# Attention with experts: five token tables instead of one, and the high parts of keys and queries copied on another engine

## The chip, the core and the metric

The kernel runs on one core of a Trainium2 chip. The metric is the device time of one launch in microseconds (us). TensorE is called PE here (its weight loads PEld), VectorE DVE, ScalarE ACT, GpSimd POOL and SyncE SP. All engines work their own instructions in order; they meet through semaphores.

## What is computed

Attention with rotary position encoding over 8 batches and 8 heads (576 tokens, head width 64) makes a table of 4608 tokens by 512. A gate picks one of 8 experts for each token, and each token goes through its expert's two layers.

```python
B, H, S, D = 8, 8, 576, 64
q_rot, k_rot = rotate(q), rotate(k)
attn = softmax(q_rot @ k_rot.T / sqrt(D))
x = (attn @ v).transpose(0, 2, 1, 3).reshape(B * S, H * D)     # 4608 x 512
e_idx = argmax(x @ w_gate, axis=1)                             # one of 8 experts
for e in range(8):
    mask = e_idx == e
    ye = maximum(x[mask] @ w1[e], 0) @ w2[e]                   # 512 -> 1024 -> 512
    out[mask] = gate_w[mask] * sigmoid(x @ w_output_gate)[mask, e] * ye
```

## The kernel before

**Attention** goes through 32 pairs of heads, four pairs to a batch. A pair has nine steps; a step makes the scores of 128 queries against 576 keys on PE (`scores`), their maximum on DVE (`peak`), the exponential on ACT (`exp`), and one step later a transpose on DVE (`turn`). The global step number is `g`; pair n has steps 9n to 9n+8. Everything else is placed at a step by the table `EVENTS`, written by hand: an entry (name, offset, slot) of pair n is issued at step 9n + offset, in slot 1 (behind the step's exponential) or slot 2 (behind its transpose). The code is issued in that order, so it is also the order on each engine.

To get ready, pair n needs: its keys and queries (`load`, one DMA of 1152 KB into the buffer `raw`, two of them); the rotation (`mult1` and `add1` for keys, `mult0` and `add0` for queries, on POOL); and a split of each into a high part, rounded to the matmul's type (`keyhi`, `queryhi`: a copy), and a low part (`keylo`, `querylo`: the difference). In the kernel before, copy and difference both run on POOL. The high and low keys are `kh` and `kl`, and `q` holds both parts of the queries. A pair's buffer `raw` comes free for the load of pair n+2 when `querylo` has read it. The values are loaded with four DMAs a pair (`loadv`), and the products with the values (`av0` to `av3`) run on PE one pair later.

**Placing.** When a batch's four pairs are done, `place` runs the gate for its 576 tokens as a list of small pieces, one a step, mostly on POOL: it writes the tokens' rows to the DRAM table `xd` (piece `s13`, eight DMAs of SP), counts them by expert, works out for each token its place in the expert's list (`pi`, piece `s17`), and writes the token's number there: five indirect DMAs of POOL (`scatter`, one for each chunk of 128 tokens, the last of 64) into the DRAM list `lst`, 36864 entries filled with a large number at the start. Since the five write one tensor, each waits for the one before to land. In the kernel before, an empty piece stands behind each scatter, so they are two steps apart.

**Experts** (`Moe`). Tokens are handled in slots of 256 or 128 tokens of one expert; the first five slots are taken from the first batches, before all tokens are placed. Three tables of slots (0, 2, 1) are made by `slots`: it works out which rows of 128 entries of `lst` a slot reads, gathers them with one indirect DMA of POOL into `tk` (a row without a token holds the large number), turns `tk` on PE (`tr`) and keeps the token numbers (`idx`). Slot s then gathers its tokens' rows `xg` from `xd` (POOL), turns them, and runs both layers; its weights are loaded by SP and split into high and low parts (`wh` on ACT, `wl` on DVE or POOL). The last batch's `place` and the tables 2 and 1 are issued in pieces between the first slots' matmuls, two pieces to each eighth of a slot, and `gather(s + 2)` stands at the seventh eighth of slot s.

Of the kernel before, what the change touches and what calls it, by code (L numbers as in the profile page):

```python
# [10 lines left out]
F32 = mybir.dt.float32  # L11
# [4 lines left out]
ALU = mybir.AluOpType  # L16
# [6 lines left out]
E, FF = 8, 1024  # L23
P = 128
# [3 lines left out]
NCH = 5  # L28
# [3 lines left out]
BIG = float(1 << 22)  # L32
# [3 lines left out]
NB, TAIL, PO = S // 32, 160, 192  # L36

EVENTS = [
    ("load", -18, 1), ("mult1", -13, 1), ("add1", -11, 1), ("mult0", -10, 1), ("add0", -9, 1), ("key", -8, 1),
    ("query", -6, 2), ("lasts", 1, 2), ("loadv", 1, 2),  # L40
    ("av0", 10, 1), ("av1", 12, 1), ("av2", 14, 1), ("av3", 16, 1),
    ("den", 10, 2), ("evict", 16, 2), ("newxb", 17, 1), ("back", 17, 1), ("divide", 17, 2),
]
# [66 lines left out]
def body(ctx, tc, nb, offs, qk, v, rope, cst, gates, w, out):  # L110
    nc = tc.nc
    NT = nb * S

    def pool(st, n, b, **k):
        return st.enter_context(tc.tile_pool(name=n, bufs=b, **k))


    early, main, scores = ExitStack(), ExitStack(), ExitStack()
    cpool = pool(ctx, "cpool", 1, side="left")
    dpool = pool(ctx, "dpool", 1, space=bass.MemoryType.DRAM)  # L120
    px, px2 = pool(ctx, "px", 1, side="left"), pool(ctx, "px2", 2, side="left")
    pa2 = pool(main, "pa", 2, side="left")
    pp1, pp2 = pool(early, "pp", 1, side="right"), pool(early, "pp2", 2, side="right")
    ps_a = pool(main, "ps_a", 1, space=PSUM, side="left")
    ps_s = pool(scores, "ps_s", 2, space=PSUM, side="right")

    small = Small(ps_s)
    pools = px, px2, pa2, pp1, pp2, ps_s, small, ps_a

    xd = dpool.tile([NT, XW], F32, name="xd")  # L130
    nl = E * list_rows(nb)
    lst = dpool.tile([nl, 1], F32, name="lst")

    first = Pair.first(tc, pools, qk[0, 0], rope)
    ident = cpool.tile([P, P], F32, name="ident")
    make_identity(nc, ident)
    o = offs[C_TRI]
    ct = cpool.tile([P, o], F32, name="ct")
    cc = lambda i: ct[:, offs[i]:offs[i + 1]]

    stage = pa2.tile([P, 2, S], F32, tag="stage", name="stage", bufs=1).rearrange("p a b -> p (a b)")
    nst = offs[-1] - o
    sc = lambda i: stage[:, offs[i] - o:offs[i + 1] - o]

    ii = cpool.tile([P, NP, 2, HW], F32, name="ii")
    trib = cpool.tile([P, P], BF16, name="trib")
    oneb = cpool.tile([P, P], BF16, name="oneb")
    cnt = cpool.tile([P, E], F32, name="cnt")
    zero, big = stage[:, nst:nst + 256], stage[:, nst + 256:nst + 256 + nl // P]
    nc.vector.memset(zero, 0.0)  # L150
    nc.vector.memset(big, BIG)
    nc.scalar.dma_start(out=ct, in_=cst[:, 0:o])
    nc.scalar.dma_start(out=stage[:, 0:nst], in_=cst[:, o:])
    nc.scalar.dma_start(out=ii[:, :, :, D:], in_=gates)

    def consts():
        for h in range(2):
            nc.vector.tensor_copy(ii[:, :, h, 0:D], ident[:, h * D:h * D + D].unsqueeze(1).broadcast_to((P, NP, D)))
        nc.vector.tensor_copy(trib, sc(C_TRI))
        nc.vector.tensor_copy(oneb, sc(C_ONE))  # L160
        nc.vector.memset(cnt, 0.0)
        nc.sync.dma_start(out=lst.rearrange("(p n) o -> p (n o)", p=P), in_=big)

    att = Attention(tc, nb, pools, cc, ident, ii, first, trib, oneb, cnt, zero, qk, v, xd, lst)
    n0 = slot_counts(nb)[0]
    moe = Moe(tc, nb, (px, px2, small), cc, ident, cnt, w, xd, lst, out)

    if n0:
        g = att.done(nb - 3) + 1
        for k, f in enumerate(pieces(moe.table0(), 14)):  # L170
            att.at(g + k, 2, f)
        att.at(att.done(nb - 2) - att.nplace + 22, 2, moe.fetch)
    att.start(consts)
    for g in range(att.G):
        att.step(g)
    early.close()
    if n0:
        moe.open_right(pool(ctx, "mr", 1, side="right", reuse_waits="tile"))
        moe.begin0()
    for g in range(att.G, att.G + TURN):  # L180
        att.step(g)
    scores.close()
    small.move(pool(ctx, "ps_x", 2, space=PSUM, side="right", reuse_waits="tile"))
    if not n0:
        att.rest(lambda g: True)
        main.close()
        moe.open_right(pool(ctx, "mr", 1, side="right", reuse_waits="tile"))
        left = []
    else:
        att.rest(lambda g: g <= att.G + 7)  # L190
        moe.begin1()
        att.rest(lambda g: True)
        main.close()
    moe.open_left(pool(ctx, "ml", 1, side="left", reuse_waits="tile"),
                  pool(ctx, "ps_m", 1, space=PSUM, side="left", reuse_waits="tile"))
    if n0:

        a, b, n = att.last, pieces(moe.table1(), 60), len(att.last) - 10
        left = a[:n] + [lambda f=f, g=g: (f(), g()) for f, g in zip(a[n:], b)] + b[10:]
    else:  # L200
        for f in att.last + pieces(moe.table1(), 60):
            f()
        moe.fetch()
        moe.begin0()
        moe.begin1()
    moe.run(left)


def pieces(gen, n):

    return [lambda: next(gen, None) for _ in range(n)]


class Attention:


    def __init__(self, tc, nb, pools, cc, ident, ii, first, trib, oneb, cnt, zero, qk, v, xd, lst):
        nc = tc.nc
# [10 lines left out]
        for i in range(2):  # L229
            o = (pp1.tile([P, 2, P], F32R, name=f"bd{i}"), px.tile([P, 2 * NCH], F32, name=f"z{i}"),  # L230
                 px.tile([P, 2 * NCH], F32, name=f"rz{i}"))
# [18 lines left out]

        for n, pr in enumerate(self.pairs):
            g, b = 9 * n, n // NP
            fs = {"load": pr.load, "key": pr.key, "query": pr.query, "lasts": pr.lasts, "loadv": pr.loadv, "den": pr.den, "evict": pr.evict, "back": pr.back,
                  "newxb": lambda pr=pr, b=b: newxb(b) if pr.hp == 0 else None}
            fs["divide"] = lambda pr=pr, b=b: pr.divide(xbs[b])
            for t in range(2):
                fs[f"mult{t}"] = lambda pr=pr, t=t: pr.mult("P", t)
                fs[f"add{t}"] = lambda pr=pr, t=t: pr.add("P", t)
            for k, (b0, b1) in enumerate(PIECES):
                fs[f"av{k}"] = lambda pr=pr, b0=b0, b1=b1: [pr.values(j) for j in range(b0, b1)]  # L260
            for name, o, k in EVENTS:
                if n > 1 or name not in ("load", "mult1", "add1", "key", "mult0", "add0", "query")[:7 if n == 0 else 1]:
                    at(g + o, k, fs[name])
            if n % NP == NP - 1:
                fs = place(tc, (px, px2, small), b, NT, cc, trib, oneb, cnt, xbs, xd, lst)
                self.nplace = len(fs)
                if b == nb - 1:
                    self.last = fs
                else:
                    for k, f in enumerate(fs):  # L270
                        at(g + PLACE + k, 2, f)
# [43 lines left out]
class Pair:  # L315
# [79 lines left out]
    def keylo(self, eng):  # L395
        self.sub(eng, self.kl, self.raw[:, 2, :], self.kh.bitcast(F32))

    def key(self):
        self.keyhi("P")
        self.keylo("P")  # L400

    def queryhi(self, eng, x=slice(0, S)):
        if x.start == 0:

# [6 lines left out]
    def lasts(self):  # L411

        for h in range(2):
            r = slice(h * D, h * D + D)
            self.nc.scalar.copy(self.bd[r, :, r], self.q.bitcast(F32)[r, :, QM:S])

    def query(self):
        self.queryhi("P")
        self.querylo("P")

    def begin(self):
        self.pc, self.ps, self.m = {}, {}, {}
# [95 lines left out]
def place(tc, pools, b, NT, cc, trib, oneb, cnt, xbs, xd, lst):  # L518

    nc = tc.nc  # L520
# [3 lines left out]
    V = nc.vector if last else nc.gpsimd  # L524
    tt = V.tensor_tensor
    b3 = lambda t: t.unsqueeze(2).broadcast_to((P, NCH, E))
    T = {}
# [94 lines left out]
    def scatter(c):  # L622
        m = QR if c == 2 else P
        nc.gpsimd.indirect_dma_start(  # L624
            out=lst[:, :], out_offset=bass.IndirectOffsetOnAxis(ap=T["pi"][:m, c:c + 1], axis=0),
            in_=T["tok"][:m, c:c + 1], in_offset=None, bounds_check=E * list_rows(NT // S) - 1, oob_is_err=False)

    def both(f, c):
# [2 lines left out]
    if last:  # L631
        fs = [s0, s1, s2, s3, s4, s5, s6, s7, s8, both(s9, 1), both(s10, 2), both(s11, 3), both(s12, 4), s13, s14, s15, s16, s17]
# [3 lines left out]
        fs = [s0, s1, s2, no, no, s3, no, no, s4, s5, s6, s7, no, no, s8, both(s9, 1), both(s10, 2), both(s11, 3),  # L636
              lambda: add(4), no, no, s12, s13, no, no, s14, s15, no, no, s16, s17]
    for c in range(NCH):
        fs += [lambda c=c: scatter(c), lambda: None]
    return fs  # L640


class Moe:
# [24 lines left out]
    def t(self, sh, n, dt=F32):  # L668
        return self.p1.tile(sh, dt, name=n)
# [14 lines left out]
    def slots(self, n, m, ends, delta, first, step, wait):  # L684
# [19 lines left out]
        if first is not None:  # L704
            V.tensor_tensor(out=row, in0=row, in1=first, op=ALU.add)

        tk = t([m, P], f"{n}tk")
        V.memset(tk, BIG)
        yield
        V.tensor_copy(ri, row)  # L710
        yield
        self.nc.gpsimd.indirect_dma_start(
            out=tk, out_offset=None, in_=self.lst.rearrange("(r c) o -> r (c o)", c=P),
            in_offset=bass.IndirectOffsetOnAxis(ap=ri[0:m, :], axis=0), bounds_check=E * self.rows - 1, oob_is_err=False)
        for _ in range(wait):
            yield
        tr = self.small.tile(f"{n}tr2")
        idx = self.idx[n] = t([P, m], f"{n}idx", I32)
        self.nc.tensor.transpose(out=tr[:, 0, 0:m], in_=tk, identity=self.ident[0:m, 0:m])
# [331 lines left out]
```

## Time and profile before

| | |
|---|---|
| time, median of 3 runs (lowest to highest) | 1294.99 us (1290.09 to 1308.81) |
| profiled execution: its time, and its span | 1298.8 us, 1296.9 us |
| mean granted TensorE clock | 0.889 |
| busy: PE, DVE, ACT, POOL | 1096.8, 838.9, 605.7, 622.8 us |
| attention (first scores to last product) | about 23 to 764 us of the span |
| experts | about 768 us to the end |

The profile's span is the stretch of the profiled execution that its instructions cover. A wait is put down to the instruction of another engine that came last; "issue" is a wait for nothing that the profile shows. A row of the timeline has start, duration (us), engine, line, operation and its tiles, the count, and in brackets the idle time before it and what ended it. A row of the windows has the stretch, and for each engine its busy time and count, then PE's granted clock, the share of 16 DMA engines that was busy, and the GB/s.

### The profile page before, as it was taken

The page shows a single profiled execution, that of the slowest core. Times are in us where ns is not written, and L with a number is a line of the kernel's source. Part 1 is how long each engine was busy: PE and PEld are TensorE (multiplying, and loading weights), DVE is VectorE, ACT ScalarE, POOL GpSimd, SP SyncE. Part 2 cuts the span into 40 slices and gives each one's busy share as a digit, 9 for nine tenths or more (in the row PEclk, how much of TensorE's full clock was granted, in tenths as well). Part 3 has the DMA queues.
Part 4 walks back from the last instruction along what each step waited for, and adds up shares of the span by engine and source line. Part 5 has one row for each costly group of instructions (what it writes and reads, how often), then busy time and mean ns, then how long its engine had stood idle before and what let it go on. Part 6 is the DMA issues. An engine that isn't in the chain of part 4 may idle for free.

```text
span 1296.9 us, 34609 instructions
## 1 busy us (share of the span) xinstructions
PE 1096.8 (85%) x14419; PEld 932.1 (72%) x14419; DVE 838.9 (65%) x1295; ACT 605.7 (47%) x1247; POOL 622.8 (48%) x570
## 2 busy tenths in 40 slices
PE   3988977887886886987985879829999999999998
PEld 2777766675765665765764668628988898989897
DVE  6888855664775674764674546616667767676784
ACT  2455533433443432442432433414557667676674
POOL 6766746636847646656645022122224334363342
PEclk9999977877998887886777779859999999999999
DMA  7454865863865945855852878956668878888891
GB/s 233 126 149 112 120 127 92 114 130 60 146 138 111 143 80 110 125 98 111 116 106 38 108 210 96 249 126 218 208 203 318 267 238 309 292 282 295 278 338 44
DMA packets 88288, 216.19 MB, mean 167 GB/s; under 512 B 48157, under 2 KB 48444, under 8 KB 80064
## 3 DMA queue, kind: packets, MB, share of 16 engines
q1 hardware_dynamic: 78880, 194.18, 62.5%
q0 software_dynamic: 7776, 18.94, 4.8%
q8 instruction: 115, 1.88, 0.8%
q10 hardware_dynamic: 1472, 0.82, 0.2%
q14 instruction: 45, 0.37, 0.1%
HBM read 195.89 MB, written 20.11 MB: 167 GB/s over the span
## 4 chain that ended last, share of the span: by engine, by line
PE 48%; issue 13%; DMA 10%; POOL 6%; DVE 5%; ACT 1%; POOLq 0%; DVEq 0%; ACTq 0%
PE py L928 14%; PE ph L900 11%; PE acc L482 8%; DMA lst<-tok,pi 7%; PE sc L442 7%; PE ph L890 4%; PE acc L501 2%; POOL raw L383 2%; DVE pt L463 2%; POOL lst L624 1%; PE mtp L872 1%; DVE m L448 1%; DMA out<-y,0idx 1%; DVE wl L858 1%; PE sc L435 1%
## 5 line engine op out<-in xcount | busy, mean ns | idle before, releaser
L457 ACT ACTIVATE pm<-sc,m 128x576 f32<-128x576 f32 x288 | 213.2, 740 | 327.5 <-DVE m L448 324.5
L448 DVE TENSOR_REDUCE m<-sc 128x1 f32<-128x576 f32 x288 | 213.9, 743 | 170.1 <-PE sc L442 113.9
L482 PE MATMUL acc<-pt,v 32*64 32x128 f32 (+1 forms) x9216 | 256.9, 331 | 76.7 <-issue 44.0
L858 DVE TENSOR_TENSOR wl<-wr,wh 128x1024 fp32r<-128x1024 f32 x183 | 251.6, 1386 | 72.5 <-ACT wh L856 70.7
L482 PEld LDWEIGHTS acc<-pt,v 32*64 32x64 f32 x9216 | 194.9, 150 | 120.4 <-issue 69.4
L442 PE MATMUL sc<-kh,q 64*128 64x288 f32 x1024 | 240.0, 358 | 48.5 <-ACT pm L457 19.4
L442 PEld LDWEIGHTS sc<-kh,q 64*128 64x128 f32 x1024 | 169.3, 218 | 95.2 <-ACT pm L457 35.4
L463 DVE STREAM_TRANSPOSE pt<-pm 128x576 f32<-128x576 f32 x288 | 220.5, 766 | 3.9 <-ACT pm L457 2.9
L856 ACT CAST wh<-wr 128x1024 fp32r<-128x1024 f32 x208 | 213.3, 1051 | 19.3 <-DMA wr<-in_w 19.3
L928 PE MATMUL py<-wh,ht 128*128 128x512 f32 x640 | 217.8, 405 | 3.2 <-ACT ht L902 2.2
L900 PE MATMUL ph<-xt,wh 128*128 128x256 f32 x896 | 164.4, 286 | 7.6 <-ACT xb L514 4.5
L383 POOL TENSOR_TENSOR raw<-raw,rt 128x1152 f32<-128x1152 f32 x62 | 164.1, 2647 | 9.8 <-DMA raw<-in_qk 9.0
L900 PEld LDWEIGHTS ph<-xt,wh 128*128 128x128 f32 x896 | 141.3, 193 | 9.8 <-ACT xb L514 4.8
L928 PEld LDWEIGHTS py<-wh,ht 128*128 128x128 f32 x640 | 122.5, 192 | 28.8 <-ACT ht L902 2.4
L928 PE MATMUL py<-wl,ht 128*128 128x512 f32 x320 | 127.3, 398 | 2.8 <-POOL wl L858 2.8
L624 POOL DMA_INDIRECT lst<-tok,pi x40 | 41.4, 1035 | 181.1 <-DMA lst<-tok,pi 177.5
L900 PE MATMUL ph<-xt,wl 128*128 128x256 f32 x448 | 127.5, 285 | 0.0
L442 PE MATMUL sc<-kl,q 64*128 64x288 f32 x512 | 121.0, 326 | 0.0
L858 POOL TENSOR_TENSOR wl<-wr,wh 128x1024 fp32r<-128x1024 f32 x25 | 60.8, 2433 | 89.0 <-ACT wh L856 82.9
L442 PEld LDWEIGHTS sc<-kl,q 64*128 64x128 f32 x512 | 96.7, 220 | 0.0
L387 POOL TENSOR_TENSOR raw<-raw 128x576 f32<-128x576 f32 x62 | 87.8, 1415 | 2.2
L900 PEld LDWEIGHTS ph<-xt,wl 128*128 128x128 f32 x448 | 86.3, 193 | 0.0
(205 smaller groups left out, 1299.5 us busy)
## 6 DMA issues: line engine op xcount, KB each, us to landing
wr<-in_w SPq DMA_DIRECT2D x208, 512.0 KB, 5.4
v<-in_v SPq DMA_DIRECT2D x128, 288.0 KB, 7.6
raw<-in_qk SPq DMA_DIRECT2D x31, 1152.0 KB, 8.5
xd<-xb SPq DMA_DIRECT2D x32, 224.0 KB, 9.9
raw<-in_qk SPq DMA_DIRECT2D x2, 576.0 KB
xd<-xb SPq DMA_DIRECT2D x16, 65.0 KB, 2.7
xd<-xb SPq DMA_DIRECT2D x8, 112.0 KB, 11.4
lst<-tok,pi POOLq DMA_INDIRECT x40, 8.1
```

Of the source, the lines that this page charges most:

```text
L383: self.eng(eng).tensor_tensor(out=rv, in0=rv, in1=self.rt[:, 2 * t:2 * t + 2, x], op=ALU.mult)
L387: self.eng(eng).tensor_tensor(out=r[:, 2 * t, x], in0=r[:, 2 * t, x], in1=r[:, 2 * t + 1, x], op=ALU.add)
L442: nc.tensor.matmul(ps[:, a, :HS], self.q[r, w, c * P:c * P + P], mov[r, a * HS:a * HS + HS], start=(n == 0), stop=(n == 2))
L448: nc.vector.tensor_reduce(self.m[i], ps[:, :, :HS], axis=AX.XY, op=ALU.max, negate=True)
L457: nc.scalar.activation(pe.rearrange("p (a b) -> p a b", a=2), self.ps[i][:, :, :HS], AF.Exp, bias=self.m[i], scale=1.0, accum_out=self.z[: ...
L463: self.nc.vector.transpose(out=self.pt[:, st[0] + 5 * st[1] if st else 4, :], in_=self.pc.pop(i))
L482: nc.tensor.matmul(self.acc[h * D:h * D + D, a, o:o + 32 * n], self.v[r, h, j, :], self.pt[r, u:u + n, 32 * j:32 * j + 32], start=(j == 0) ...
L624: nc.gpsimd.indirect_dma_start(out=lst[:, :], out_offset=bass.IndirectOffsetOnAxis(ap=T["pi"][:m, c:c + 1], axis=0), in_=T["tok"][:m, c:c ...
L856: self.nc.scalar.copy(wh, r)
L858: eng.tensor_tensor(out=wl, in0=r, in1=wh.bitcast(F32), op=ALU.subtract)
L900: nc.tensor.matmul(ph[:, f, :], st[:, dc, fs], mv[:, dc, :], start=(n == 0), stop=(n == 11))
L928: self.nc.tensor.matmul(py[h], st[:, f, hs], mv, start=(f == 0 and n == 0), stop=(f == 7 and n == 2))
```

## The change

The one list becomes five, one for each chunk of a batch; a scatter of chunk c writes list c only. Readers gather the same rows from all five into five tiles and take the least on DVE, since a place that a list does not hold reads as the large number. The five tiles are filled on POOL instead of DVE. The empty piece behind each scatter is gone, so they are one step apart. The copies that make the high parts run on ACT, the differences stay on POOL, and the steps of both are given one by one.

```diff
-    ... ("add0", -9, 1), ("key", -8, 1), ("query", -6, 2), ...
+    ... ("add0", -8, 1), ("kh", -7, 1), ("kl", -6, 1), ("qh", -5, 1), ("ql", -4, 1), ...
...
-    lst = dpool.tile([nl, 1], F32, name="lst")
+    lst = [dpool.tile([nl, 1], F32, name=f"lst{c}") for c in range(NCH)]
...
-        nc.sync.dma_start(out=lst.rearrange("(p n) o -> p (n o)", p=P), in_=big)
+        for l in lst:
+            nc.sync.dma_start(out=l.rearrange("(p n) o -> p (n o)", p=P), in_=big)
...
-            fs = {..., "key": pr.key, "query": pr.query, ...
+            fs = {..., "kh": lambda pr=pr: pr.keyhi("A"), "kl": lambda pr=pr: pr.keylo("P"),
+                  "qh": lambda pr=pr: pr.queryhi("A"), "ql": lambda pr=pr: pr.querylo("P"), ...
...
     def scatter(c):
-            out=lst[:, :], out_offset=bass.IndirectOffsetOnAxis(ap=T["pi"][:m, c:c + 1], axis=0),
+            out=lst[c][:, :], out_offset=bass.IndirectOffsetOnAxis(ap=T["pi"][:m, c:c + 1], axis=0),
...
-        fs += [lambda c=c: scatter(c), lambda: None]
+        fs += [lambda c=c: scatter(c)]
...
-        tk = t([m, P], f"{n}tk")
-        V.memset(tk, BIG)
+        tks = [t([m, P], f"{n}tk{c}") for c in range(NCH)]
+        for tk in tks:
+            self.nc.gpsimd.memset(tk, BIG)
...
-        self.nc.gpsimd.indirect_dma_start(
-            out=tk, out_offset=None, in_=self.lst.rearrange("(r c) o -> r (c o)", c=P), ...
+        for l, tk in zip(self.lst, tks):
+            self.nc.gpsimd.indirect_dma_start(
+                out=tk, out_offset=None, in_=l.rearrange("(r c) o -> r (c o)", c=P), ...
         for _ in range(wait):
             yield
+        tk = tks[0]
+        for o in tks[1:]:
+            V.tensor_tensor(out=tk, in0=tk, in1=o, op=ALU.min)
```

On POOL, at the scatters of the first batch, the order before was this, from the second scatter on (`raw`, `kh`, `kl` and `q` carry buffer numbers; `dd` is a piece of the next batch's gate; L383 and L387 are the rotation's products and sums):

```order
L624 DMA lst<-tok_2226,pi_2514 36864x1
L387 TENSOR_TENSOR raw_2378<-raw_2378 128x576
L383 TENSOR_TENSOR raw_2378<-raw_2378,rt 128x1152
L624 DMA lst<-tok_2226,pi_2514 36864x1
L387 TENSOR_TENSOR raw_2378<-raw_2378 128x576
L361 CAST kh_2738<-raw_2378 128x576
L367 TENSOR_TENSOR kl_2739<-raw_2378,kh_2738 128x576
L624 DMA lst<-tok_2226,pi_2514 36864x1
L543 TENSOR_TENSOR dd_2770<-lgs_2684,mx_2746 128x40
L624 DMA lst<-tok_2226,pi_2514 36864x1
L361 CAST q_2827<-raw_2378 128x576
L367 TENSOR_TENSOR q_2827<-raw_2378,q_2827 128x576
```

With the change POOL has there, from the first scatter on (line numbers of the changed file):

```order
L619 DMA lst_84<-tok_2233,pi_2522 36864x1
L370 TENSOR_TENSOR q_2535<-raw_2073,q_2535 128x576
L386 TENSOR_TENSOR raw_2385<-raw_2385,rt 128x1152
L619 DMA lst_85<-tok_2233,pi_2522 36864x1
L619 DMA lst_86<-tok_2233,pi_2522 36864x1
L390 TENSOR_TENSOR raw_2385<-raw_2385 128x576
L619 DMA lst_87<-tok_2233,pi_2522 36864x1
L386 TENSOR_TENSOR raw_2385<-raw_2385,rt 128x1152
L619 DMA lst_88<-tok_2233,pi_2522 36864x1
L390 TENSOR_TENSOR raw_2385<-raw_2385 128x576
L538 TENSOR_TENSOR dd_2780<-lgs_2697,mx_2753 128x40
L370 TENSOR_TENSOR kl_2777<-raw_2385,kh_2776 128x576
```

The scatters go to five lists and stand closer together, between the rotation's instructions of one pair instead of around it and the split; the two copies (CAST) are gone from POOL.

On ACT, in a pair in the middle of the attention, from the exponential of its third step on (`pm`, `sc`, `m` with the step's number), before:

```order
L457 ACTIVATE pm_2_4317,z_107<-sc_2_4308,m_2_4315 128x576
L457 ACTIVATE pm_3_4333,z_107<-sc_3_4324,m_3_4331 128x576
L457 ACTIVATE pm_4_4388,z_107<-sc_4_4379,m_4_4386 128x576
L457 ACTIVATE pm_5_4400,z_107<-sc_5_4391,m_5_4398 128x576
L457 ACTIVATE pm_6_4450,z_107<-sc_6_4441,m_6_4448 128x576
```

and in the same place with the change:

```order
L452 ACTIVATE pm_2_4321,z_111<-sc_2_4312,m_2_4319 128x576
L362 CAST kh_4323<-raw_3933 128x576
L452 ACTIVATE pm_3_4340,z_111<-sc_3_4331,m_3_4338 128x576
L452 ACTIVATE pm_4_4393,z_111<-sc_4_4384,m_4_4391 128x576
L362 CAST q_4395<-raw_3933 128x576
L452 ACTIVATE pm_5_4407,z_111<-sc_5_4398,m_5_4405 128x576
```

The next pair's two copies now stand behind the third and the fifth exponential.

On POOL, where table 0 (`0tk`, gathered with the row numbers `0ri`) is read during the sixth batch's scatters, stood before, from the fourth scatter on:

```order
L624 DMA lst<-tok_8421,pi_8716 36864x1
L543 TENSOR_TENSOR dd_9001<-lgs_8912,mx_8976 128x40
L712 DMA 0tk<-lst,0ri 10x128
L624 DMA lst<-tok_8421,pi_8716 36864x1
L361 CAST q_9061<-raw_8573 128x576
```

and with the change, from that batch's second scatter on:

```order
L619 DMA lst_85<-tok_8428,pi_8748 36864x1
L619 DMA lst_86<-tok_8428,pi_8748 36864x1
L709 DMA 0tk_8769<-lst_84,0ri 10x128
L709 DMA 0tk_8770<-lst_85,0ri 10x128
L709 DMA 0tk_8771<-lst_86,0ri 10x128
L709 DMA 0tk_8772<-lst_87,0ri 10x128
L709 DMA 0tk_8773<-lst_88,0ri 10x128
L390 TENSOR_TENSOR raw_8600<-raw_8600 128x576
L619 DMA lst_87<-tok_8428,pi_8748 36864x1
```

Five gathers stand behind the third scatter of that batch, ahead of a sum of the rotation and the last two scatters.

More of the change, by code (lines that the diff above doesn't have):

```diff
@@ L38 @@
 EVENTS = [
-    ("load", -18, 1), ("mult1", -13, 1), ("add1", -11, 1), ("mult0", -10, 1), ("add0", -9, 1), ("key", -8, 1),
-    ("query", -6, 2), ("lasts", 1, 2), ("loadv", 1, 2),
[2 rows of a table added]
     ("av0", 10, 1), ("av1", 12, 1), ("av2", 14, 1), ("av3", 16, 1),
@@ L196, in body @@
     if n0:
-        a, b, n = att.last, pieces(moe.table1(), 60), len(att.last) - 10
-        left = a[:n] + [lambda f=f, g=g: (f(), g()) for f, g in zip(a[n:], b)] + b[10:]
+        a, b, n = att.last, pieces(moe.table1(), 60), len(att.last) - NCH
+        left = a[:n] + [lambda f=f, g=g: (f(), g()) for f, g in zip(a[n:], b)] + b[NCH:]
     else:
@@ L252, in __init__ @@
             g, b = 9 * n, n // NP
-            fs = {"load": pr.load, "key": pr.key, "query": pr.query, "lasts": pr.lasts, "loadv": pr.loadv, "den": pr.den, "evict": pr.evict, "back": pr.back,
+            fs = {"load": pr.load, "kh": lambda pr=pr: pr.keyhi("A"), "kl": lambda pr=pr: pr.keylo("P"),
+                  "qh": lambda pr=pr: pr.queryhi("A"), "ql": lambda pr=pr: pr.querylo("P"), "lasts": pr.lasts, "loadv": pr.loadv, "den": pr.den, "evict": pr.evict, "back": pr.back,
                   "newxb": lambda pr=pr, b=b: newxb(b) if pr.hp == 0 else None}
@@ L261, in __init__ @@
             for name, o, k in EVENTS:
-                if n > 1 or name not in ("load", "mult1", "add1", "key", "mult0", "add0", "query")[:7 if n == 0 else 1]:
+                if n > 1 or name not in ("load", "mult1", "add1", "kh", "kl", "mult0", "add0", "qh", "ql")[:9 if n == 0 else 1]:
                     at(g + o, k, fs[name])
@@ L396, in keylo @@
         self.sub(eng, self.kl, self.raw[:, 2, :], self.kh.bitcast(F32))
-    def key(self):
-        self.keyhi("P")
-        self.keylo("P")
     def queryhi(self, eng, x=slice(0, S)):
@@ L415, in lasts @@
             self.nc.scalar.copy(self.bd[r, :, r], self.q.bitcast(F32)[r, :, QM:S])
-    def query(self):
-        self.queryhi("P")
-        self.querylo("P")
     def begin(self):
@@ L711, in slots @@
         yield
-        self.nc.gpsimd.indirect_dma_start(
-            out=tk, out_offset=None, in_=self.lst.rearrange("(r c) o -> r (c o)", c=P),
-            in_offset=bass.IndirectOffsetOnAxis(ap=ri[0:m, :], axis=0), bounds_check=E * self.rows - 1, oob_is_err=False)
+        for l, tk in zip(self.lst, tks):
+            self.nc.gpsimd.indirect_dma_start(
+                out=tk, out_offset=None, in_=l.rearrange("(r c) o -> r (c o)", c=P),
+                in_offset=bass.IndirectOffsetOnAxis(ap=ri[0:m, :], axis=0), bounds_check=E * self.rows - 1, oob_is_err=False)
         for _ in range(wait):
             yield
+        tk = tks[0]
+        for o in tks[1:]:
+            V.tensor_tensor(out=tk, in0=tk, in1=o, op=ALU.min)
         tr = self.small.tile(f"{n}tr2")
```

2 rows, old and new, of the table EVENTS are left out of this document.

## The prediction

> **What bounds the kernel now.** I read the page's busy table first, then the waits, then windows of the attention and the experts.
>
> ```profile
> PE 1096.8 (85%) x14419; PEld 932.1 (72%) x14419; DVE 838.9 (65%) x1295; ACT 605.7 (47%) x1247; POOL 622.8 (48%) x570
> POOL lst L624 <- DMA lst<-tok,pi: 177.5, 29, 11.2
> PE acc L482 <- issue: 44.0, 23, 4.9
> PE acc L482 <- DVE m L448: 15.1, 5, 3.8
> PE sc L442 <- POOL q L361: 9.9, 4, 2.8
> PE 0tr L719 <- DMA 0tk<-lst,0ri: 9.9, 1, 9.9
> PE mtp L872 <- DMA xg<-xd,0idx: 23.4, 1, 23.4
> ```
>
> PE is the busiest engine, and POOL stands still for 177.5 us, 29 times, for one thing: a scatter into the list waits for the scatter before it. Whether that costs time is read from the pairs. A pair makes nine transposes (L463), so a window's count over nine is its number of pairs (columns: stretch, DVE's busy time of that line and count, clock, DMA share, GB/s):
>
> ```profile
> 58.60:164.20 105.60, 41.32 (x54) 1.00 0.59 130
> 164.20:750.20 586.00, 164.90 (x216) 0.80 0.64 111
> ```
>
> Six pairs ahead of the first scatter take 105.6 / 6 = 17.6 us each at full clock. The 24 pairs from the first scatter on take 586 / 24 = 24.4 us at a mean clock of 0.80. So 586 - 24 x 17.6 = **163.6 us** are lost there. The first six pairs include most of a batch's placing work (all of it but the scatters and the pieces right ahead of them), so that work is not the loss.
>
> How a scatter reaches PE, in the third batch (POOL's rows, then PE's):
>
> ```profile
> 376.93 1.01 POOL L624 DMA_INDIRECT lst<-tok,pi  x1 [7.62 <-DMA lst<-tok,pi]
> 386.30 0.94 POOL L624 DMA_INDIRECT lst<-tok,pi  x1 [4.32 <-DMA lst<-tok,pi]
> 397.55 0.99 POOL L624 DMA_INDIRECT lst<-tok,pi  x1 [5.31 <-DMA lst<-tok,pi]
> 398.54 0.68 POOL L361 CAST q<-raw 128x576 fp32r<-128x576 f32 x1
> 399.28 0.53 PE L442 MATMUL sc<-kh,q 64*128 64x288 f32 x2 [2.71 <-POOL q L361]
> ```
>
> Behind the fifth scatter stands the copy of the next pair's queries, and PE waits for it. After a stop PE runs at half clock although it is always busy (columns: stretch, PE, PEld, DVE, ACT, POOL busy, clock, DMA share, GB/s):
>
> ```profile
> 195.00:200.00 5.00, 1.89 (x63) 1.55 (x69) 3.45 (x7) 1.74 (x5) 1.45 (x3) 0.93 0.30 64
> 200.00:205.00 5.00, 5.00 (x57) 4.01 (x64) 1.67 (x3) 0.83 (x2) 0.17 (x1) 0.50 0.04 3
> 205.00:210.00 5.00, 5.00 (x96) 4.29 (x88) 2.34 (x4) 1.23 (x4) 2.96 (x3) 0.50 0.04 3
> 210.00:215.00 5.00, 5.00 (x73) 4.00 (x58) 3.25 (x7) 3.04 (x9) 4.82 (x6) 0.71 0.98 48
> ```
>
> Going through PE's rows between 164 and 750 us I count 15 places with a gap of 2.5 us or more (two gaps less than 9 us apart are one place). The first and the last:
>
> ```profile
> 172.24 2.43 PE L482 MATMUL acc<-pt,v 32*64 32x128 f32 x61 [4.86 <-issue]
> 733.66 0.52 PE L482 MATMUL acc<-pt,v 32*64 32x160 f32 x11 [3.08 <-issue]
> ```
>
> Their gaps add up to 69.8 us; with the slow clock behind each, a place costs 163.6 / 15 = **10.9 us**. Four are the wait for `q` above, one is the wait for table 0, and ten are "issue" in the middle of the products with the values: PE is out of instructions, always during or right behind a burst of DMAs. Five of the ten come up to 16 us behind a batch's stores to `xd`; the other five behind loads that the late POOL had held back. SP's rows show both kinds of traffic ahead of the first places, and its longest wait in total:
>
> ```profile
> 151.98 1.02 SPq L597 DMA_DIRECT2D xd<-xb  x2
> 170.36 0.36 SPq L372 DMA_DIRECT2D raw<-in_qk  x1
> 186.37 1.71 SPq L378 DMA_DIRECT2D v<-in_v  x4
> SPq L372 <- POOL q L367: 287.3, 23, 30.6
> ```
>
> **The change, part by part.** *The lists.* The 177.5 us of waits go: no scatter writes what the one before wrote, and the same list's last scatter is a batch away (4 x 17.6 = 70 us, against 8.1 us to land, below). POOL keeps the issue of 1.0 us each, and can issue one indirect DMA right behind another, as it does for `xg`:
>
> ```profile
> 748.17 1.00 POOL L834 DMA_INDIRECT xg<-xd,0idx  x1 [0.31 <-issue]
> 749.47 1.00 POOL L834 DMA_INDIRECT xg<-xd,0idx  x1 [0.30 <-issue]
> ```
>
>  Of the 15 places, the four for `q` go. Of the five behind held-back loads I take four as gone, since loads go out late when `querylo` is late. The five behind the stores stay: the stores are the same. Table 0 stays. So 8 places, 8 x 10.9 = **87 us**; bounds: 4 places (44 us) and 14 (153 us).
>
> *The experts' first slots.* In the row of waits, PE stands 23.4 us for `xg`, whose gather POOL issues behind the last batch's five scatters. It waits for one `wl` behind the batch before's:
>
> ```profile
> 788.01 0.50 PE L928 MATMUL py<-wl,ht 128*128 128x512 f32 x1 [2.82 <-POOL wl L858]
> 870.00:876.00 6.00, 6.00 (x20) 4.75 (x19) 2.00 (x3) 1.70 (x3) 3.81 (x4) 0.57 0.39 130
> ```
>
> Both go, and with them about 2 us of the 6 at a clock of 0.57: 23.4 + 2.8 + 2 = **28 us** (bounds 0 and 40). What is late next is the wait of a store to `out` for the store before it, which is untouched.
>
> *The copies.* The 62 copies leave POOL, and come on ACT:
>
> ```profile
> L361 POOL CAST kh<-raw 128x576 fp32r<-128x576 f32 x31 | 20.6, 666 | 26.2 <-PE sc L442 25.7
> 8.55 0.67 ACT L359 CAST kh<-raw 128x576 fp32r<-128x576 f32 x1 [1.02 <-DVE raw L387]
> 79.59 0.19 ACT L457 ACTIVATION_READ_ACCUMULATOR pm<-sc,m 128x1 f32 x1
> 80.41 0.74 ACT L457 ACTIVATE pm<-sc,m 128x576 f32<-128x576 f32 x1 [0.62 <-DVE m L448]
> 82.53 0.19 ACT L457 ACTIVATION_READ_ACCUMULATOR pm<-sc,m 128x1 f32 x1
> 83.25 0.74 ACT L457 ACTIVATE pm<-sc,m 128x576 f32<-128x576 f32 x1 [0.53 <-DVE m L448]
> ```
>
> One takes 0.67 us on ACT, as on POOL. It stands behind the third and the fifth exponential of a pair, where ACT idles 0.62 and 0.53 us before the next: 0.05 + 0.14 us too little, times 31 pairs = 6 us lost (bounds: 0, if the step had slack, and 62 x 0.67 = 42). POOL's 41 us less are worth nothing by themselves, since it is not the bound of a quiet pair. But the copy adds waits both ways. ACT waits for POOL's sums, and behind it stand the exponentials, so DVE's transposes and PE's scores; POOL's differences wait for ACT, so POOL can no longer run a pair ahead. Cover: from the difference of the queries to the next pair's query sum POOL needs
>
> ```profile
> L383 POOL TENSOR_TENSOR raw<-raw,rt 128x1152 f32<-128x1152 f32 x62 | 164.1, 2647 | 9.8 <-DMA raw<-in_qk 9.0
> L387 POOL TENSOR_TENSOR raw<-raw 128x576 f32<-128x576 f32 x62 | 87.8, 1415 | 2.2
> raw<-in_qk SPq DMA_DIRECT2D x31, 1152.0 KB, 8.5
> lst<-tok,pi POOLq DMA_INDIRECT x40, 8.1
> ```
>
> 1.4 + 2 x 2.65 + 2 x 1.4 = 9.5 us of a pair's 17.6, so 8.1 us are left; five scatters take 5 of them, once a batch. The load of `raw`, freed by a difference, takes 8.5 us and is wanted a pair later. I take nothing for the waits; without the cover it is a rival below.
>
> *The readers.* Each table is five gathers instead of one, and four minima on DVE, next to its 0.15 us copies: 0.6 us.
>
> ```profile
> L712 POOL DMA_INDIRECT 1tk<-lst,1ri x1 | 1.7, 1683 | 9.7 <-DMA wr<-in_w 9.7
> L712 POOL DMA_INDIRECT 0tk<-lst,0ri x1 | 1.0, 972 | 7.1 <-DMA lst<-tok,pi 7.1
> ```
>
> Table 2 has sixteen pieces between gather and use, which hide four more of 1 to 1.7 us. Table 1 has four pieces, as before: four gathers more are 4 to 7 us that PE and DVE wait, with the minima 7 us. For table 0 I change nothing: the 9.9 us of before were a wait for scatters, and now its third gather waits for a scatter issued right before it, 8.1 us, and two more follow. Filling four more lists at the start is 576 KB ahead of nothing that the first scores need: 1 us (0 to 3).
>
> **Sum**, against the profiled execution's own 1298.8 us: -87 - 28 + 6 + 7 + 1 = -101, so 1198. The median of the runs shown lies 3.8 us under the profiled one: **1194 us**.
>
> Two rules of the skill speak to single terms. The Trainium skill, "TensorE: Matmul & The Clock Gate", Part 1, says that about 3.4 us of sustained matmuls bring the full clock back; the rows from 200 to 210 us show 0.50 for 10 us of busy PE, so the trace does not agree here, and I price a place by the rows. The Trainium skill, "DMA: Bandwidth & Descriptors", section "Issuing engines are not separate DMA queues", says that all DMAs run on the same 16 engines, which speaks against five scatters at once; no run here shows two scatters in flight, and the third rival has that case.
>
> **Rivals.**
> 1. *The stores' places go too.* If PE starves only when loads and stores pile up behind a late POOL, only table 0's place stays: 153 + 28 - 14 = 167 less, **1128 us**. For it: the first six pairs show no place. Against: the first place, at 167 us, lies ahead of the first wait of a scatter.
> 2. *Only the `q` places go*, all ten "issue" places staying: 44 + 28 - 14 = 58 less, **1237 us**. For it: loads and `v` still go out in one burst a pair, now closer together. Or a place gives back its gap alone (69.8 / 15 = 4.7 us) because the clock falls for another reason: 8 x 4.7 + 28 - 14 = 51 less, **1244 us**. The rows of the clock speak against it. This is the case in which the Trainium skill's rule on the clock, named above, would hold.
> 3. *Scatters in flight together land one behind the other.* A scatter alone in the window from 200 us keeps 0.04 x 16 = 0.6 of an engine busy. If the three that table 0 waits for share one engine, they land after 24 us instead of 8: PE waits 16 us longer, and about 5 at the slow clock: **1215 us**.
> 4. *Slower: ACT waits for POOL's sums in each pair.* If POOL's 9.5 us and its wait for ACT and for a late `raw` fill more than a pair's 17.6, each copy holds the exponentials. To reach 1321 (2% over before) it takes (1321 - 1194) / 31 = 4.1 us a pair, so it decides once POOL's chain is 8.1 + 4.1 = 12 us late in every pair. Against: nothing in a quiet pair adds to it. **1325 us**.
> 5. *The change does not do what it says*: a scatter still waits for the last, through some shared wait. Then the copies and readers alone count, +14: **1309 us**. Against: gathers `xg` go out 1.3 us apart in the rows above.
>
> **Chances**: forecast 0.55 (its own range 1155 to 1230), first rival 0.15, second 0.17, third 0.07, fourth 0.04, fifth 0.02. About 2% is what a measurement of this kernel can tell from no change. Everything below 1269 is faster by more: the forecast and the first three rivals but for the slowest edge, 0.93; within 2%, 0.04; slower, 0.03. The range for 8 in 10 reaches from the first rival's edge to past the second: **1130 to 1250**.
>
> **What would show it.** POOL's row of 177.5 us is gone and L619 of the changed file waits for pieces of `place` alone. From the first scatter on, pairs take about 20 us; PE shows some seven places, most of them behind the stores. No wait of PE for POOL's `q`; a short one for ACT's copy would be the fourth rival's beginning. `mtp` waits no longer for `xg`; `1tr` waits some 6 us. The forecast is wrong if the clock stays near 0.80 without gaps, if ACT waits for POOL's sums by more than 30 us in all, or if the "issue" places move with the new times of the loads to be as many as before.

## The result, and the profile after

The changed kernel takes **1253.8 us** (median of 4 runs, 1251.5 to 1277.5), the kernel before on the same chip 1297.4 us (1290.1 to 1308.8): a ratio of 0.965, with a 95% interval of 0.957 to 0.972. Ratios here and below leave out executions that took over 1.5% more than the fastest of their kernel. The forecast was 1194 us with a range of 1130 to 1250. The sign was right, and the gain is 43.5 us where 101 were forecast.

The execution profiled with these runs was the slowest of them (1277.5 us). The lines below are from a second profile of the changed kernel (e5), with a span of 1251.3 us, which stands beside the median. It ran on another chip, where the kernel before takes 1318.6 us, so a difference between it and the trace of before holds that of the chips too. Its busy engines, and from its waits those that the prediction spoke of:

```profile
PE 1066.3 (85%) x14419; PEld 911.7 (73%) x14419; DVE 836.8 (67%) x1304; ACT 639.3 (51%) x1309; POOL 602.1 (48%) x535
...
POOL kl L370 <- ACT kh L362: 149.1, 30, 13.2
POOL q L370 <- ACT q L362: 65.1, 25, 9.5
PE acc L477 <- issue: 47.1, 19, 5.8
PE 0tr L719 <- DVE 0tk L716: 20.4, 1, 20.4
PEld 1tr L719 <- issue: 5.3, 1, 5.3
```

The row of 177.5 us is gone, as forecast, and so is PE's wait for POOL's `q`. POOL now idles for ACT's copies, 214 us in all, and PE, ACT and DVE show no wait for POOL on that account. But PE is still out of instructions in the middle of the value products, for 47.1 us (44.0 before). The windows show where the time stayed (the transposes of L458, then clock, DMA share and GB/s):

```profile
165.00:724.00 559.00, 165.38 (x216) 0.84 0.68 115
219.60:236.90 17.30, 6.89 (x9) 1.00 0.45 128
```

A quiet pair takes 17.3 us, as before. The 24 pairs from the first scatter on take 559.0 us where they took 586.0. Counted as in the prediction, PE has 11 places in them instead of 15: the four waits for `q` are gone, the ten "issue" places are still ten, and table 0's has grown from 9.9 to 20.4 us. The loss is 559.0 - 24 x 17.6 = 137 us, so 12.4 us a place (10.9 before). **These pairs gave back 27 us where 87 were forecast.**

How that splits into a number and a price is not firm. The slowest execution, on the chip of before, has in the same window:

```profile
166.00:736.00 570.00, 165.38 (x216) 0.79 0.65 112
```

There the same counting finds 8 places, one more than the seven of the forecast, but a loss of 570.0 - 24 x 17.6 = 148 us, 18 us a place. The gaps of 2 us or more add up to 69.8 us before (the figure of the prediction), to 70.0 in e5 and to 58.1 in this execution. So the 27 us of e5 came from what is lost beside the gaps, with the mean clock up from 0.80 to 0.84, and a count of gaps above 2.5 us differs between executions of one kernel.

### What a stop of PE looks like

The first place, in PE's rows and in SP's ahead of it:

```profile
167.41 0.77 PE L477 MATMUL acc<-pt,v 32*64 32x160 f32 x23
173.21 1.15 PE L477 MATMUL acc<-pt,v 32*64 32x128 f32 x28 [5.03 <-issue]
```

```profile
152.23 0.36 SPq L594 DMA_DIRECT2D xd<-xb  x1
...
156.47 0.52 SPq L375 DMA_DIRECT2D raw<-in_qk  x1
159.26 6.51 SPq L381 DMA_DIRECT2D v<-in_v  x4
```

The view of the DMAs has a queue q8 of the kind "instruction": 115 packets, 1.88 MB. PE has 2 x 14419 rows of matmuls and weight loads, so 65 bytes go with each: by its size this queue brings PE's instructions, 16 KB at a time. The same view for 164 to 170 us, then for 170 to 172 us (packets, MB, share of the 16 engines):

```profile
q1 hardware_dynamic: 200, 1.32, 97.1%
q14 instruction: 1, 0.01, 0.3%
```

```profile
q1 hardware_dynamic: 77, 0.47, 90.1%
q8 instruction: 1, 0.02, 4.1%
```

While data fills the engines no packet of q8 starts for 6 us; then one does, lands at 171.8 us by the packets' records, and PE runs on at 173.2. Of the 19 "issue" stops of 1.2 us or more from 165 to 735 us, 12 end 1.2 to 2.2 us after such a packet has landed; the other seven end 2.8 us or more after one. That the packets end the stops is read from this order of times and was not tested by itself. The Trainium skill, "Runtime: NRT & Kernel Launch", "Instruction fetch mechanics", says that instructions come in 16 KiB blocks over a DMA queue of their own, which agrees with these packets, and that this cost is mostly hidden; the stop of 5.03 us shows where it is not.

### What a scatter does to everybody else

The first scatter of the second batch, and the load of `raw` behind it (POOL's and SP's rows):

```profile
262.61 1.09 POOL L619 DMA_INDIRECT lst<-tok,pi  x1 [0.29 <-POOL pi L615]
```

```profile
265.17 0.35 SPq L375 DMA_DIRECT2D raw<-in_qk  x1
```

The DMAs from 266 to 272 us, and from 273 to 276 us:

```profile
DMA packets 31, 0.29 MB, mean 48 GB/s; under 512 B 0, under 2 KB 0, under 8 KB 0
...
q1 hardware_dynamic: 31, 0.29, 108.2%
```

```profile
DMA packets 199, 1.07 MB, mean 356 GB/s; under 512 B 84, under 2 KB 84, under 8 KB 84
...
q1 hardware_dynamic: 130, 1.04, 99.1%
```

The records have all 16 engines taken in both stretches. In the first, a packet of 9216 bytes takes 16 x 6 x 1.082 / 31 = 3.4 us; in the second 16 x 3 x 0.991 / 130 = 0.37 us. For 7 to 10 us (once 18) behind a batch's first scatter, and again behind the scatters that were queued meanwhile, every transfer stands nearly still. The trace of before has such stretches too, behind scatters with a load under way. By the packets' records the stretches in which packets take 2.5 us or more add up to 107 us ahead of 780 us before, to 117 us in e5 and to 111 in the slowest execution: the change took POOL's waits away and left these. I had read those 8.1 us as the scatter's own time to land, hence as a matter for POOL, which waited for it. They are everybody's.

### The profile page after: what moved, and what is told of

It is laid out like the page before. It is cut to its first block, busy times and chain, and to the rows that moved or that the text cites. A ratio compares the mean times of both kernels' runs of the same rounds, so it can differ in the third digit from the quotient of the medians.

```text
span 1275.7 us, 34743 instructions
## 1 busy us (share of the span) xinstructions
PE 1106.6 (87%) x14419; PEld 938.8 (74%) x14419; DVE 836.9 (66%) x1304; ACT 640.2 (50%) x1309; POOL 602.5 (47%) x535
## 3 DMA queue, kind: packets, MB, share of 16 engines
q8 instruction: 115, 1.88, 0.8%
## 4 chain that ended last, share of the span: by engine, by line
PE 53%; issue 10%; DVE 8%; ACT 5%; DMA 4%; another core or an unknown queue 2%; POOL 1%; SPq 0%; POOLq 0%; ACTq 0%; DVEq 0%
PE py L928 13%; PE ph L900 11%; PE acc L477 10%; PE sc L437 9%; PE ph L890 4%; PE acc L496 3%; DMA wr<-in_w 2%; DVE pt L458 2%; ACT pm L452 2%; DVE wl L858 2%; DVE m L443 2%; PE mtp L872 1%; PE sc L430 1%; ACT wh L856 1%
## 5 line engine op out<-in xcount | busy, mean ns | idle before, releaser
L477 PE MATMUL acc<-pt,v 32*64 32x128 f32 (+1 forms) x9216 | 269.3, 337 | 59.2 <-issue 37.8
L477 PEld LDWEIGHTS acc<-pt,v 32*64 32x64 f32 x9216 | 201.8, 152 | 108.5 <-issue 70.8
L458 DVE STREAM_TRANSPOSE pt<-pm 128x576 f32<-128x576 f32 x288 | 220.6, 766 | 1.2 <-ACT pm L452 0.3
L900 PEld LDWEIGHTS ph<-xt,wh 128*128 128x128 f32 x896 | 143.2, 195 | 15.1 <-DVE ht L903 7.2
L370 POOL TENSOR_TENSOR kl<-raw,kh 128x576 fp32r<-128x576 f32 x31 | 43.8, 1411 | 164.3 <-ACT kh L362 160.7
L496 PE MATMUL acc<-ii,ac 128*128 128x160 f32 (+1 forms) x320 | 71.1, 370 | 31.4 <-ACT ac L486 30.4
```

The source lines that it names most:

```text
L458: self.nc.vector.transpose(out=self.pt[:, st[0] + 5 * st[1] if st else 4, :], in_=self.pc.pop(i))
L477: nc.tensor.matmul(self.acc[h * D:h * D + D, a, o:o + 32 * n], self.v[r, h, j, :], self.pt[r, u:u + n, 32 * j:32 * j + 32], start=(j == 0) ...
L496: self.nc.tensor.matmul(self.out(c, n), self.ac[:, c, :, :].rearrange("p a x -> p (a x)")[:, 0:n], self.ii[:, self.hp, :, :].rearrange("p ...
L900: nc.tensor.matmul(ph[:, f, :], st[:, dc, fs], mv[:, dc, :], start=(n == 0), stop=(n == 11))
```

## The experiments

Five theories. **A**: PE stops where its next instructions come late behind other DMAs; its causes are the stores to `xd`, the loads, or (D) the scatters. **B**: the lists gave what was forecast, and the copies on ACT ate half. **C**: the clock falls by itself. **D**: the 4-byte writes of a scatter that lie close together are taken slowly by the memory, and other transfers stand meanwhile. **D2**: any scatter of 4-byte elements costs this, wherever it writes.

The medians of the kernel before are 1297 to 1358 us on the chips used, which differ by more than the change is worth. So ratios to it are compared, above all within a group (one chip), and expected times are read as ratios to 1297. "Stretch" is the window of pairs 8 to 31 with its 216 transposes, in the profiled execution, which took up to 10 us more than the median of its kernel (e1). The diffs are cut to the lines that matter.

| group | kernel | ratio to before (95%) | stretch, us |
|---|---|---|---|
| 1 | e1, lists alone | 0.970 (0.962 to 0.979) | 602.7 |
| 1 | e2, copies alone | 0.985 (0.978 to 0.991) | 624.2 |
| 1 | e3, wide stores | 0.917 (0.908 to 0.926) | 528.9 |
| 1 | e4, without 30 loads of `v` | 0.928 (0.922 to 0.934) | 536.0 |
| 2 | e5, the change again | 0.954 (0.944 to 0.964) | 559.0 |
| 2 | e6, permuted lists | 0.928 (0.917 to 0.939) | 517.6 |
| 2 | e7, permuted lists and wide stores | 0.882 (0.874 to 0.889) | 478.0 |
| 2 | e8, kernel before, permuted list | 0.940 (0.930 to 0.949) | 539.2 |
| 3 | e9, as e7, table 0 waits longer | 0.865 (0.858 to 0.872) | 488.0 |
| 3 | e10, as e9, products in seven pieces | 0.886 (0.878 to 0.895) | 509.8 |
| 3 | e11, kernel before with both | 0.873 (0.863 to 0.883) | 502.6 |
| 3 | e12, as e9, table 1 waits longer | 0.869 (0.862 to 0.876) | 482.0 |
| 4 | e13, kernel before, same places | 1.003 (0.998 to 1.008) | 627.5 |
| 4 | e14, two groups | 0.950 (0.940 to 0.961) | 574.4 |
| 4 | e15, four groups | 0.924 (0.916 to 0.933) | 547.4 |
| 4 | e16, sixteen bytes apart | 0.939 (0.931 to 0.947) | 570.4 |

### e1 and e2: each half of the change alone

```diff
 # e1: five lists; copies and their places as before
-"kh": lambda pr=pr: pr.keyhi("A")   ...   "qh": lambda pr=pr: pr.queryhi("A")
+"kh": lambda pr=pr: pr.keyhi("P")   ...   "qh": lambda pr=pr: pr.queryhi("P")
 # e2, against the kernel before: the copies on ACT at their new places; one list
-    ... ("key", -8, 1), ("query", -6, 2), ...
+    ... ("kh", -7, 1), ("kl", -6, 1), ("qh", -5, 1), ("ql", -4, 1), ...
```

> The five lists and their readers alone; the high parts are copied by POOL at the places of before. Theory A (PE's instructions come late: its next 16 KB of them arrive over the queue q8 behind other DMAs, and PE stops in the value products wherever that happens; who copies does not matter): 1245 to 1262 us, as the whole change, with as many issue places. Theory B (the lists gave what was forecast, and the copies on ACT with their waits both ways ate half of it): 1195 to 1215 us. Theory C (the clock falls by itself in the second third of the run, whatever the waits): 1245 to 1262 us, with half clock in stretches that no stop precedes.

> The copies on ACT and their new places alone; one list as before. Theory A: the waits of the scatters stay and the places with them: 1285 to 1305 us, as before; the wait for xg stays at 20 us or more. Theory B: slower than before by what the copies ate, 1330 us or more.

The lists alone give 0.970, most of the change, and not the 0.92 to 0.94 of theory B. The copies alone are not slower: B falls from both sides. Whether they help stays open: 0.985 rests on three of ten executions, the medians of all give 0.995, and A expected 0.99 to 1.006. So it is not shown either that the two parts add up to the whole change.

### e3 and e4: fewer pieces in the stores, fewer loads

```diff
 # e3: values of all heads side by side in xb, gates behind them
-for i in range(n):
-    nc.sync.dma_start(out=rows[:, i, 0:DM - D] ..., in_=x[:, i, 0:DM // D * HW - HW] ...)
-nc.sync.dma_start(out=rows[:, :, DM - D:], in_=x[:, :, H * HW - HW:H * HW - 15])
+nc.sync.dma_start(out=rows, in_=xbs[b][0:m, c:c + n, 0:XW])
 # e4: loadv returns early
+if self.n > 1:
+    self.v = Pair.vs[self.n % 2]; return
```

> The changed kernel, but each pair's division writes the values of all heads side by side and the gates behind them, so that a batch's stores to xd go out in 3 DMAs of 2052 bytes a piece instead of 8 with 256 and 260 bytes a piece: the same bytes, an eighth of the pieces; DVE and ACT get 4 small operations a pair more. Theory A with the stores as the main cause: most of the places behind stores go, 1195 to 1225 us. Theory A with the loads as the main cause: 1240 to 1255 us. Theories B and C: 1250 to 1262 us.

> The changed kernel without 30 of the 32 loads of v (each pair takes the v of the first pair with its parity): half of the attention's loads, 35 MB, are gone. Theory A with the loads as the main cause: nearly all places go, 1110 to 1190 us. Theory A with the stores as the main cause: the places right behind the stores stay, 1200 to 1240 us. Theories B and C: 1245 to 1262 us.

The packets of the changed kernel (e5), and of e3:

```profile
DMA packets 89249, 216.88 MB, mean 173 GB/s; under 512 B 48481, under 2 KB 49404, under 8 KB 81024
```

```profile
DMA packets 56355, 216.89 MB, mean 175 GB/s; under 512 B 10977, under 2 KB 11900, under 8 KB 48128
```

The same bytes in fewer pieces, with four small operations a pair more on DVE and on ACT: 0.917, a little under what theory A has with the stores as a main cause (0.92 to 0.945). B and C expected the change's own time. Taking away 35 MB of loads, 16% of all bytes, gains no more than gathering the 9.5 MB of stores into larger pieces: 0.928 is in A's range for the stores, not for the loads. e3 also has three store DMAs a batch in place of eight; the length of the pieces and the number of DMAs were not told apart. But two stretches of slow packets a batch stayed in both, each behind scatters. That gave theory D.

### e5 to e8: the same scatters to other places

```diff
-V.tensor_copy(new("pi", [P, NCH], I32), T["po"])
+W.tensor_copy(pi, T["po"])                       # W = nc.vector
+W.tensor_scalar(a, pi, 7, 4, op0=ALU.bitwise_and, op1=ALU.logical_shift_left)
+W.tensor_scalar(r, pi, 3, 15, op0=ALU.logical_shift_right, op1=ALU.bitwise_and)
+W.tensor_scalar(pi, pi, -128, None, op0=ALU.bitwise_and)
+W.tensor_tensor(out=a, in0=a, in1=r, op=ALU.bitwise_or)
+W.tensor_tensor(out=pi, in0=pi, in1=a, op=ALU.bitwise_or)
```

A slot reads a row of 128 entries as a set, so their order within the row is free.

> The changed kernel once more, beside the next three on one chip: all theories expect 0.96 to 0.97 of before, pairs 8 to 31 of the attention at 23 to 25 us in the mean, and two or three stretches of 7 to 10 us behind each batch's scatters in which every packet of the loads takes 2.5 us or more.

> The changed kernel, but the place of a token in its row of 128 list entries is permuted: neighbours in rank are written 16 entries apart, not side by side (six small integer operations a batch on DVE). Same number of scatters, elements and bytes. Theory D (a scatter's 4-byte writes side by side are taken one after another by the memory, 8 us in all, and other transfers, PE's instructions among them, stand still meanwhile): the stretches of slow packets shrink below 3 us, a scatter lands in 3 us or less, most places go: 0.87 to 0.92 of before. Theory D2 (any scatter of 4-byte elements costs this, wherever it writes): 0.96 to 0.97, stretches as before. Theory A with the stores as the main cause: 0.96 to 0.97.

> The permuted list and the stores of 2052 bytes together. Theory D: the two causes add up, pairs 8 to 31 at 17.5 to 18.5 us, 0.84 to 0.88 of before. Theory D2: as the wide stores alone, 0.91 to 0.92.

> The kernel before, one list, copies on POOL, with the permuted list alone. Theory D: a scatter lands in 3 us or less, so the waits of scatters fall from 177 us to under 60 and the stretches go: 0.88 to 0.93 of before; the five lists are then worth little. Theory D2: 0.99 to 1.01.

With permuted lists the change takes 1217.6 us in place of 1253.6 (medians). The stretches of slow packets add up to 48 us, where e5 has 117; most are 3 to 5 us long, and five "issue" places are left of ten. With the wide stores too, 1164.0 us. The windows of pairs 8 to 31 of e6 and of e7:

```profile
169.90:687.50 517.60, 165.25 (x216) 0.86 0.65 121
```

```profile
169.00:647.00 478.00, 164.97 (x216) 0.92 0.53 132
```

The clock goes up as the stops go (0.84, 0.86, 0.92), which C has no room for. The kernel before gains as much from the permutation alone (0.940) as from the five lists and the copies (0.954; the intervals meet). Its waits of scatters, and their time to land:

```profile
POOL lst L631 <- DMA lst<-tok,pi: 83.7, 26, 8.3
```

```profile
lst<-tok,pi POOLq DMA_INDIRECT x40, 4.9
```

177.5 us became 83.7, and 8.1 us became 4.9. Theory D had the direction right and expected more (under 60 and 3, and ratios of at most 0.92, 0.88 and 0.93 for e6, e7 and e8): a scatter spread over its rows still takes 4.9 us.

### e9 to e12: what is left

```diff
-yield from self.slots(0, 2 * self.n0, end, dl, None, 2, 4)        # e9, e10, e12
+yield from self.slots(0, 2 * self.n0, end, dl, None, 2, 14)
-for k, f in enumerate(pieces(moe.table0(), 14)):                  # as many steps more
+for k, f in enumerate(pieces(moe.table0(), 24)):
-PIECES = ((0, 5), (5, 10), (10, 14), (14, 18))                    # e10, at steps 10 to 16
+PIECES = ((0, 3), (3, 6), (6, 9), (9, 12), (12, 14), (14, 16), (16, 18))
-yield from self.slots(1, self.n1, e1, d1, g1[:, 0:1], 1, 4)       # e12
+yield from self.slots(1, self.n1, e1, d1, g1[:, 0:1], 1, 8)
```

> The permuted list and the wide stores, and the transposes of table 0 wait 14 pieces behind its gathers instead of 4. PE stood 11.8 us for table 0 with both (and pair 29 took 29.8 us where a quiet one takes 17.4). If that stop is the gathers' latency alone: it goes, 8 to 14 us less, 0.87 to 0.875 of before. If POOL's queue holds up the pair's sums all the same: 0.88 as without it.

> As the run before, but the value products of a pair go in seven pieces of 2 or 3 blocks, one a step, in place of four pieces of 4 or 5 blocks at every second step: PE eats its instructions evenly. If what is left of the stops is PE running dry while it issues 40 products on end: 5 to 20 us less than the run before. If not: within 3 us of it, or slower, since a step's exponentials then wait behind products in each step.

> The kernel before (one list, copies on POOL) with the permuted list and the wide stores. If the five lists gain only by what a slow scatter costs, little is left for them: within 2.5% of the five lists with both (0.88), so 0.88 to 0.905. If their waits count by themselves: 0.92 or more.

> The permuted list, the wide stores, table 0 with 14 pieces, and table 1's last transposes wait 8 pieces behind its gathers instead of 4. PE stood 4.6 us for them: 3 to 6 us less than with table 0's wait alone.

PE's wait at table 0 fell from 11.8 us (e7) to 4.0 (e9). But pairs 28 to 30, around it, take no less; first e7, then e9:

```profile
562.20:630.20 68.00, 20.65 (x27) 0.88 0.32 72
```

```profile
555.10:634.70 79.60, 20.71 (x27) 0.71 0.27 62
```

So the stop was not the latency of the gathers alone; what else is held up there stays open. The ratios (0.882 and 0.865) do speak for a gain, but the two ran on different chips, and e7 has the shorter time (1164.0 us against 1171.5). e9 and e12 cannot be told apart. Smaller pieces of the products (e10) are 2 to 3% slower than e9. PE's idle time ahead of the products falls, first e9, then e10:

```profile
PE acc L477 <- issue: 21.1, 13, 3.5
PE acc L477 <- issue: 11.3, 4, 4.0
```

But a quiet pair now takes 18.4 us in place of 17.4, and what the 24 pairs take beyond quiet ones is 70 us in e9 and 68 in e10. So fewer of these stops gained nothing here. e11 is the sharpest: with both causes cured, the kernel before reaches 0.873, and the five lists with the copies 0.865 (e9, which waits longer for table 0). The intervals overlap, though all four times of e9 (1167.5 to 1175.5 us) lie below those of e11 (1176.3 to 1200.0). **Once the writes are spread and the stores are wide, some 1 to 2% is left of the gain of the change studied here, too little for these runs to tell.** e9 has the lowest ratio: 13.5% under the kernel before, 9 to 10% under the change.

### e13 to e16: is it the places?

```diff
 # k = 0 (e13), 1 (e14), 2 (e15), 5 (e16); the permuted list of e8 has k = 3
+W.tensor_scalar(a, pi, 2**k - 1, 7 - k, op0=ALU.bitwise_and, op1=ALU.logical_shift_left)
+W.tensor_scalar(r, pi, k, 2**(7 - k) - 1, op0=ALU.logical_shift_right, op1=ALU.bitwise_and)
```

> The kernel before with the same six integer operations as in the permuted list, but with numbers by which each place stays as it was. If the places count: 0.99 to 1.01 of before, a scatter lands in 8 us. If only the delay counts: 0.93 to 0.95, as with the permuted list.

> The kernel before; even and odd ranks of a row of 128 go to two halves of it, so that an expert's up to 16 tokens of a scatter write in 2 runs of 8 side by side. If the number side by side counts: between the two known points (16: 8.1 us to land; 2 in 64 bytes: 4.9), about 6.3 us, 0.96 to 0.98 of before.

> The kernel before; ranks go to four quarters of their row, so 4 runs of 4 side by side. By the same line: about 5.4 us to land, 0.945 to 0.965 of before.

> The kernel before; neighbours in rank write 4 entries (16 bytes) apart, so none is beside the one before, but 4 of them lie in the same 64 bytes. If direct neighbourhood counts: as the permuted list or better, 4.9 us or less to land, 0.93 to 0.945. If writes into the same 64 bytes count: as with four groups, about 5.4 us, 0.945 to 0.965.

The waits of scatters in e13, e14, e15 and e16, in this order:

```profile
POOL lst L631 <- DMA lst<-tok,pi: 179.2, 26, 15.7
```

```profile
POOL lst L631 <- DMA lst<-tok,pi: 115.0, 27, 9.9
```

```profile
POOL lst L631 <- DMA lst<-tok,pi: 79.6, 24, 7.9
```

```profile
POOL lst L631 <- DMA lst<-tok,pi: 102.0, 30, 10.4
```

The six operations by themselves change nothing (1.003): **the places do it.** The median landing is 6.9 us in two groups (expected 6.3), 4.5 us in four (5.4) and 4.9 us in eight (e8); the pages of e13 and e16 show none. The ratios of e14 and e15 are better than expected (0.96 to 0.98 and 0.945 to 0.965). In steps of 16 bytes, where no neighbour in rank is written beside the one before, the wait lies between two and four groups, and the time is longer than with four (1266.9 against 1245.2 us). The stretches of slow packets agree: 124, 103, 69 and 97 us in e13 to e16, ahead of 780 us. So direct neighbourhood is not what counts, and neither is the number within 64 bytes alone, by which e16 would equal e15. An expert's 16 or so tokens of a scatter lie within 256 bytes in e16, within 512 in e15. Which unit of the memory this is stays open.

## Why the prediction was right or wrong, point by point

- **The waits of the scatters go**: right, with all 177.5 us. **The copies cost 6 us on ACT**: too much; a quiet pair takes 17.3 us, as before. **Waits both ways, taken as nothing**: right. POOL's 214 us for ACT's copies is idle time of an engine that is not the bound.
- **Four places for `q` go**: right. **"Of the five behind held-back loads I take four as gone, since loads go out late when `querylo` is late"**: this is the step that failed. It took the late POOL for the cause of these five. In the trace of before, each of the five begins 2.5 to 5.2 us behind the end of a stretch of slow packets, and the change leaves these stretches (107 us before, 117 in e5). The loads go out earlier now, and then stand in the scatter's stretch, with PE's instructions beside them: of the ten "issue" places of e5, five come behind the stores, as forecast, and five around the scatters (202, 267, 286, 475 to 480 and 564 us). In e6, on the chip of e5, five of the ten are left. I had a scatter's 8.1 us in hand and put them down to one waiting engine. The slow packets were in the trace of before, and I read the scatters in the view of POOL's waits alone, not in that of the DMAs.
- **8 places x 10.9 = 87 us** measured 586.0 - 559.0 = 27. In e5 four places went instead of eight, table 0's place grew by 10 us, and a place cost 12.4 us (11.5 without that growth). In the slowest execution seven went, and the 8 left cost 18 us each, so that it gave back 16. So 10.9 us is no fixed price: in e5 the number failed, in the other execution the price. Of the ten places "in the middle of the products" two stood before scores (227 and 262 us).
- **The first slots, 28 us**, with table 1's 7 taken off: from the end of the pairs to the end of the span it was 546.7 us and is 527.3, so 19.4 less where 28 - 7 = 21 were forecast. The wait for `xg` is gone, and table 1 waits 5.3 us. Right in the sum; table 2, taken as hidden, waits 4.8 us too.
- **Sum**: -27.0 - 19.4 + 0.8 (the pairs start 0.8 us later) = -45.6, from 1296.9 to 1251.3 us of span.
- **The rivals.** The second (only the `q` places go, 1237) told the mechanism best: in e5 all ten "issue" places stayed. It was 17 us too low, about what table 0's growth (10.5) and the dearer places come to. Its other form (a place gives back its gap alone, 1244) is not borne out: in e5 the gaps stayed and the slow remainder fell. The third (scatters in flight land one behind the other) was wrong in its form: several scatters queued together share one stretch of 8 to 10 us. Its place was right: table 0 waits 20.4 us, for the third gather stands behind such a stretch (POOL waits 15.1 us for the scatter ahead of it). The last sign I had named, "issue" places that move with the new times of the loads, is what came in e5.
- **A rule that I did not weigh**: the Trainium skill, "DMA: Bandwidth & Descriptors", "Specifications", says that below 512 bytes the DMA engines read, modify and write. The stores of 256 bytes (e3) agree with it in direction. It does not account for e6 by itself: the same 4-byte writes cost less when they are spread. It would have spoken against holding POOL's wait for the whole price of a scatter.

## What to carry to other kernels

A wait row names who waits, not who is hurt: when a small transfer takes long to land, look at what the other transfers' packets take in the same microseconds. "Issue" gaps of PE in a long unrolled kernel can be a DMA matter: look at when the packets of the instruction queue land (here 12 of 19 gaps end right behind one). Before splitting a buffer so that scatters need not wait for one another, try to make each cheap: spread what it writes, and give stores long pieces.

## What the runs showed of the hardware that I had not expected

- A scatter of 128 elements of 4 bytes, written close together, slows the transfers under way, loads and PE's instructions, for 7 to 10 us: most packets of 9216 bytes take 2.5 to 6.5 us instead of 0.35. Spread over rows of 512 bytes it lands in 4.5 to 5.6 us (e15, e8, e11) instead of 8.1.
- Stores of the same bytes in an eighth of the pieces are worth 4% of this kernel (1217.6 to 1164.0 us, e6 to e7).
- By the size of the queue PE's instructions arrive in packets of 16 KB, and PE's stops of 2 to 6 us mostly end behind one. In the 5 us behind each of the ten places of e5 the clock is 0.50 to 0.52.
